# Linear attention on one core: loads cut into 16 pieces on the memory side, 128 on the partition side

## The chip, the core and the metric

The kernel runs on one core of a Trainium2 chip. The engines are TensorE (PE; its weight loads are the row PEld), VectorE (DVE), ScalarE (ACT), GpSimd (POOL) and SyncE (SP); SP computes nothing and issues the transfers, which 16 DMA engines carry out. The metric is the device time of one execution in microseconds (us), the median over several runs; lower is better.

## The reference

For each of 32 heads, q, k and v are 2048 x 128 in bf16:

```python
phi_q = jnp.where(q > 0, q + 1, jnp.exp(q)) + 1e-6
phi_k = jnp.where(k > 0, k + 1, jnp.exp(k)) + 1e-6
kv = jnp.einsum("bhsd,bhse->bhde", phi_k, v)
z = jnp.einsum("bhsd->bhd", phi_k)
num = jnp.einsum("bhqd,bhde->bhqe", phi_q, kv)
den = jnp.einsum("bhqd,bhd->bhq", phi_q, z)[..., None] + 1e-6
return num / den
```

## The kernel before

One head's q, k or v is 512 KB, contiguous in memory. `rows` (L303) lays it over the 128 partitions: partition p holds tokens 16p to 16p+15, which are 2048 elements or 4 KB, contiguous in memory and in the partition. The output goes back the same way. So a head costs three loads and one store of 512 KB each, each made of 128 pieces of 4 KB on both sides.

phi(x) is computed as max(x, 0) + min(exp(x), 1) + 1e-6. For k, ACT makes the exponential `ek_sb` (L368), POOL the positive part `rk_sb` (L372), DVE `emk_sb` = min(ek, 1) + 1e-6 (L382). Five of the 16 tiles of 128 tokens get the two halves added on POOL (L390); for the others PE multiplies both halves. PE sums phi_k by v into `kvz_ps` (L413, L320), with a column of ones beside v that gives z, and ACT copies the result to `kvs_sb` (L430). For q, PE transposes 16 tiles into `xT_ps` (L436), ACT takes the exponential `eq_sb` (L447), DVE and ACT half the positive part each, `rq_sb` (L456, L454), and DVE makes `emq_sb` (L468). PE multiplies both by `kvs_sb` into `o_ps` (L483, L484), and DVE takes the denominators (L506), their reciprocals (L512) and divides (L517, L524) into `o_sb`. The last two heads divide partly on ACT (L536).

The program is written as a list of operations, each with its engine, a key (a number in units of heads), what it reads and what it writes. Every engine runs its own operations in the order of their keys; waits follow from the reads and writes. Nothing decides the order at run time.

All loads (L361) and stores (L571) are issued by SP, in one queue, in the order of these keys:

```python
load("k", k_sb, kf, h - NBI - (1.0 if h < 3 else 1.85 if h == 3 else 1.95))
load("v", v_sb, vf, h - NBI - 0.8)
load("q", q_sb, qf, h - NBI - 0.9)
late = h + 1.0 + 0.18 * h
```

`NBI` is 6: q, k and v have six buffers each, and SP waits until a buffer's readers are done before it issues the load that fills it again. The output has ten buffers (`NBO`), and the stores fall behind their heads by `0.18 * h`, so that the loads go first. The last head but two is stored in three transfers of 51, 13 and 64 partitions (`PARTS`, L252); the last head in two, of tiles 0 to 8 and 9 to 15.

Of the kernel before, what the change touches and what calls it, by code (L numbers as in the profile page):

```python
# [7 lines left out]
P = 128  # L8
# [4 lines left out]
def _ap(base: bass.AP, elem_offset: int, dims):  # L13
    return bass.AP(base.tensor, base.offset + elem_offset, [list(base.ap[0])] + [list(d) for d in dims])
# [217 lines left out]
def bass_standalone__linear_attn_elu__prompt_kernel(  # L232
# [6 lines left out]
    B, H, S, D = q.shape  # L239
    assert D == P and S == 16 * P  # L240
    NT = 16
# [13 lines left out]
    EVEN, ODD = tuple(range(0, NT, 2)), tuple(range(1, NT, 2))  # L255
    MORE = (4, 6, 8, 10, 12, 14)
    GAP = 32
    VW = NT * D + GAP

    qf = q.rearrange("b h s d -> (b h) s d")  # L260
# [4 lines left out]
    with ExitStack() as es:  # L265
        def sb(name, shape, dt):
            return es.enter_context(nc.sbuf_tensor(name, shape, dt))

        k_sb = sb("k_sb", [P, NBI, NT * D], bf16)
        v_sb = sb("v_sb", [P, NBI, VW], bf16)  # L270
        q_sb = sb("q_sb", [P, NBI, NT * D], bf16)
# [29 lines left out]
        pl = Plan()  # L301

        def rows(x, h):  # L303
            return x[h].rearrange("(p j) d -> p (j d)", j=NT)
# [11 lines left out]
               reads=[("id0",)], writes=[("ident",)])  # L316
        pl.add("pool", -7, lambda g: g.memset(_ap(vfull, 0, [[VW, NBI], [1, GAP]]), 1.0), writes=[("vones",)])

# [32 lines left out]
        for h in range(NH):  # L351
# [3 lines left out]
            bi, b2, b3, bo = h % NBI, h % 2, h % 3, h % NBO  # L355

            def load(name, buf, src, key, h=h, bi=bi):
                dst, rws = buf[:, bi], rows(src, h)
                if name == "v":
                    dst = v_sb[:, bi, GAP:]  # L360
                pl.add("sp", key, lambda sp: sp.dma_start(dst, rws), writes=[(name, bi)] + ([("vo", bi)] if name == "v" else []), dma=(name, bi))  # L361

            load("k", k_sb, kf, h - NBI - (1.0 if h < 3 else 1.85 if h == 3 else 1.95))
            load("v", v_sb, vf, h - NBI - 0.8)
            load("q", q_sb, qf, h - NBI - 0.9)

            pl.add("act", at("ek", -2.8),
                   lambda a, bi=bi, b2=b2: a.activation(ek_sb[:, b2, :], k_sb[:, bi, :], ACT.Exp),  # L368
# [36 lines left out]
            def kv(pe, tiles, start=False, stop=False, h=h, bi=bi, b3=b3, both_of=both_of):  # L405
                for j in tiles:
                    both = j in both_of or (j in ODD and j not in ADD and h > 0)
                    for src in (emk_sb, rk_sb) if both else (rk_sb,):
                        first, fin = start and j == tiles[0] and src is (emk_sb if both else rk_sb), stop and j == tiles[-1] and src is rk_sb
                        w = src[:, b3, j * D:(j + 1) * D]  # L410
                        l = j == 0 or (j in ODD and h > 0)
                        c = GAP + j * D
                        last = pe.matmul(kvz_ps[:, 1 - l:NC], lhsT=w, rhs=v_sb[:, bi, c - l:c + D], start=first, stop=fin,  # L413
# [11 lines left out]
            if h:  # L425
                pl.add("pool", h + 0.6, lambda g, bi=bi: g.memset(_ap(vfull, bi * VW + GAP + D - 1, [[2 * D, NT // 2], [1, 1]]), 1.0),
                       reads=[("v", bi)], writes=[("vo", bi)], kind="vo")
# [187 lines left out]
```

## Time and profile before

| | |
|---|---|
| median of 3 runs | 168.16 us (167.96 to 168.21) |
| the profiled execution | 167.82 us |
| its span, first to last instruction | 166.5 us |
| PE / DVE / ACT / POOL busy | 156.0 / 152.3 / 155.0 / 106.3 us |
| granted TensorE clock, mean | 0.997 |
| moved by DMA | 67.25 MB, mean 404 GB/s over the span |
| read from / written to memory | 50.33 / 16.78 MB |

Busy times are of the profiled execution. A share of DMA is the time of its packets as a share of 16 engines; packets of one engine overlap a little, so it can pass 1. "Issue to landing" is the time from SP's instruction to the last of a transfer's 16 semaphore increments.

### The profile page before, as it was taken

How to read it: one execution, taken by the hardware profiler on the slowest of the kernel's cores; microseconds unless marked ns; L12 is line 12 of the kernel's file. 1: busy time of each engine (PE TensorE's matmuls, PEld its weight loads, DVE VectorE, ACT ScalarE, POOL GpSimd, SP SyncE). 2: the span in 40 equal slices, each digit the busy share in tenths (PEclk: the TensorE clock that was granted, in tenths of full speed). 3: DMA queues.
4: the chain of work that ended last, by engine and by line, in shares of the span. 5: the costliest groups of instructions: out<-in, count | busy, mean ns of one | idle time of the engine just before them, and what ended most of it. 6: DMA issues, size and time to landing. Idle time of an engine off the chain costs nothing.

```text
span 166.5 us, 6269 instructions
## 1 busy us (share of the span) xinstructions
PE 156.0 (94%) x2819; PEld 145.3 (87%) x2453; DVE 152.3 (91%) x270; ACT 155.0 (93%) x143; POOL 106.3 (64%) x128
## 2 busy tenths in 40 slices
PE   7789999999999999999999999999999999999960
PEld 0259999999999999899999989999998999999950
DVE  0587999999999999999999999999999999999991
ACT  3979999999999999999999999999999999998790
POOL 2405788676767877676778867676787767677300
PEclk9999999999999999999999999999999999999998
DMA  5999999999999999999999999999999999999986
GB/s 205 345 417 421 413 415 419 412 407 418 417 416 419 422 417 417 422 421 411 424 420 414 423 421 415 419 421 415 422 420 416 422 421 418 418 421 418 415 310 239
DMA packets 18605, 67.25 MB, mean 404 GB/s; under 512 B 2082, under 2 KB 2210, under 8 KB 18594
## 3 DMA queue, kind: packets, MB, share of 16 engines
q1 hardware_dynamic: 18592, 67.12, 99.4%
q8 instruction: 5, 0.08, 0.2%
q14 instruction: 6, 0.05, 0.1%
q10 hardware_dynamic: 2, 0.00, 0.0%
HBM read 50.33 MB, written 16.78 MB: 403 GB/s over the span
## 4 chain that ended last, share of the span: by engine, by line
DVE 58%; PE 17%; POOL 12%; ACT 6%; issue 3%; DMA 2%; DVEq 0%
DVE o_sb L524 20%; POOL rk_sb L390 12%; DVE rq_sb L456 11%; DVE emk_sb L382 10%; DVE emq_sb L468 9%; PE kvz_ps L413 6%; PE o_ps L483 5%; PE o_ps L484 5%; ACT ek_sb L368 3%; DVE rden_sb L512 3%; DVE o_sb L517 3%; ACT eq_sb L447 2%; DMA k_sb<-in_k_dram 2%; DVE den_sb L506 2%; DVE rk_sb L390 1%
## 5 line engine op out<-in xcount | busy, mean ns | idle before, releaser
L413 PE MATMUL kvz_ps<-v_sb,rk_sb 128*128 128x129 bf16 (+1 forms) x512 | 67.0, 220 | 2.8 <-DVE rk_sb L390 1.0
L524 DVE TENSOR_TENSOR o_sb<-o_ps,rden_sb 128x768 bf16<-128x768 f32 (+2 forms) x62 | 67.8, 1135 | 0.0
L390 POOL TENSOR_TENSOR rk_sb<-rk_sb,emk_sb 128x640 bf16<-128x640 bf16 x30 | 41.9, 1395 | 39.5 <-DVE emq_sb L468 38.2
L372 POOL TENSOR_SCALAR rk_sb<-k_sb 128x1024 bf16<-128x1024 bf16 (+1 forms) x60 | 64.1, 1068 | 2.5 <-DMA k_sb<-in_k_dram 2.5
L483 PE MATMUL o_ps<-kvs_sb,emq_sb 128*128 128x129 bf16 (+1 forms) x536 | 65.2, 217 | 0.0
L484 PE MATMUL o_ps<-kvs_sb,rq_sb 128*128 128x129 bf16 (+1 forms) x536 | 64.4, 217 | 0.0
L368 ACT ACTIVATE ek_sb<-k_sb 128x2048 bf16<-128x2048 bf16 x32 | 61.0, 1907 | 2.6 <-DMA k_sb<-in_k_dram 2.6
L447 ACT ACTIVATE eq_sb<-xT_ps 128x2048 bf16<-128x2048 bf16 (+1 forms) x33 | 60.0, 1821 | 2.0 <-PE xT_ps L436 2.0
L413 PE MATMUL kvz_ps<-v_sb,emk_sb 128*128 128x129 bf16 (+1 forms) x338 | 53.3, 221 | 0.6 <-DVE emk_sb L382 0.3
L413 PEld LDWEIGHTS kvz_ps<-v_sb,rk_sb 128*128 128x128 bf16 x512 | 46.1, 98 | 7.6 <-POOL rk_sb L390 2.7
L483 PEld LDWEIGHTS o_ps<-kvs_sb,emq_sb 128*128 128x128 bf16 x536 | 51.2, 98 | 0.8 <-issue 0.3
L484 PEld LDWEIGHTS o_ps<-kvs_sb,rq_sb 128*128 128x128 bf16 x536 | 51.3, 98 | 0.0
L436 PE MATMUL xT_ps<-ident,q_sb 128*128 128x128 bf16 x512 | 33.8, 219 | 0.6 <-DMA q_sb<-in_q_dram 0.4
L436 PEld LDWEIGHTS xT_ps<-ident,q_sb 128*128 128x128 bf16 x512 | 29.9, 98 | 5.1 <-DMA q_sb<-in_q_dram 4.2
L413 PEld LDWEIGHTS kvz_ps<-v_sb,emk_sb 128*128 128x128 bf16 x338 | 32.5, 98 | 0.9 <-DVE emk_sb L382 0.5
L320 PE MATMUL kvz_ps<-ones_sb,rk_sb 128*128 128x1 bf16 x232 | 31.3, 165 | 0.0
L454 ACT ACTIVATE rq_sb<-xT_ps 128x1024 bf16<-128x1024 bf16 x30 | 30.9, 1029 | 0.0
L382 DVE TENSOR_SCALAR emk_sb<-ek_sb 128x2048 bf16<-128x2048 bf16 x32 | 22.0, 688 | 5.6 <-ACT ek_sb L368 5.6
L456 DVE TENSOR_SCALAR rq_sb<-xT_ps 128x1024 bf16<-128x1024 bf16 x34 | 23.3, 690 | 1.1 <-PE o_ps L484 1.0
L468 DVE TENSOR_SCALAR emq_sb<-eq_sb 128x2048 bf16<-128x2048 bf16 x32 | 22.1, 690 | 0.0
L320 PE MATMUL kvz_ps<-ones_sb,emk_sb 128*128 128x1 bf16 x121 | 19.9, 166 | 0.0
L430 ACT ACTIVATE kvs_sb<-kvz_ps 128x129 bf16<-128x129 f32 x32 | 9.0, 281 | 1.6 <-PE kvz_ps L413 0.9
(28 smaller groups left out, 49.2 us busy)
## 6 DMA issues: line engine op xcount, KB each, us to landing
k_sb<-in_k_dram SPq DMA_DIRECT2D x32, 512.0 KB, 15.0
q_sb<-in_q_dram SPq DMA_DIRECT2D x32, 512.0 KB, 15.1
v_sb<-in_v_dram SPq DMA_DIRECT2D x32, 512.0 KB, 15.1
out_dram<-o_sb SPq DMA_DIRECT2D x30, 512.0 KB, 15.3
out_dram<-o_sb SPq DMA_DIRECT2D x1, 288.0 KB, 3.7
out_dram<-o_sb SPq DMA_DIRECT2D x1, 256.0 KB
out_dram<-o_sb SPq DMA_DIRECT2D x1, 224.0 KB, 3.6
out_dram<-o_sb SPq DMA_DIRECT2D x1, 204.0 KB
```

The costliest lines, as they stand in the source:

```text
L320: return pe.add_instruction(mybir.InstMatmult(start_tensor_calc=start, stop_tensor_calc=stop, ldweights=False, bass_skip_group_check=True, ...
L368: lambda a, bi=bi, b2=b2: a.activation(ek_sb[:, b2, :], k_sb[:, bi, :], ACT.Exp),
L372: pl.add(eng, key, lambda e: e.tensor_scalar(rk_sb[:, b3, c], k_sb[:, bi, c], BIG, 0.0, op0=ALU.min, op1=ALU.max), reads=[("k", bi)] + ([( ...
L382: lambda d, b2=b2, b3=b3: d.tensor_scalar(emk_sb[:, b3, :], ek_sb[:, b2, :], 1.0, EPS, op0=ALU.min, op1=ALU.add),
L390: return e.tensor_tensor(out=a, in0=a, in1=b, op=ALU.add)
L413: last = pe.matmul(kvz_ps[:, 1 - l:NC], lhsT=w, rhs=v_sb[:, bi, c - l:c + D], start=first, stop=fin, skip_group_check=True)
L436: last = pe.transpose(xT_ps[:, j * P:(j + 1) * P], q_sb[:, bi, j * P:(j + 1) * P], ident[:])
L447: halves[part] = pl.add("act", key, lambda a: a.activation(eq_sb[:, b2, c], xT_ps[:, c], ACT.Exp), reads=both[part:part + 1] or both, writ ...
L456: f = lambda d: d.tensor_scalar(rq_sb[:, b3, c], xT_ps[:, c], 0.0, None, op0=ALU.max)
L483: pe.matmul(o_ap, lhsT=emq_sb[:, b3, t * P:(t + 1) * P], rhs=kvs_sb[:, b3, c0:c1], start=True, stop=False)
L484: return pe.matmul(o_ap, lhsT=rq_sb[:, b3, t * P:(t + 1) * P], rhs=kvs_sb[:, b3, c0:c1], start=False, stop=True)
L524: pl.add("dve", key, lambda d: d.tensor_tensor(out=o_sb[:, bo, 3 * g0:3 * g1, :].rearrange("p (a b) d -> p a b d", b=3), in0=_ap(full, bas ...
```

## The change

The loads of q, k and v are issued with an access pattern of their own on each side. In memory a head is now 16 pieces of 32 KB (`READS` = 16), each of which is what 8 neighbouring partitions hold; on the partition side there are 128 pieces of 4 KB as before. The same bytes go to the same places. The instruction is made directly (`InstDMACopy`), so that the two patterns stay as written. The stores are unchanged, and on every engine the instructions, their order and their waits are the same; lines below L258 move by 1, those below the load by 8.

```diff
     GAP = 32
+    READS = 16
     VW = NT * D + GAP
...
             def load(name, buf, src, key, h=h, bi=bi):
-                dst, rws = buf[:, bi], rows(src, h)
-                if name == "v":
-                    dst = v_sb[:, bi, GAP:]
-                pl.add("sp", key, lambda sp: sp.dma_start(dst, rws), writes=[(name, bi)] + ([("vo", bi)] if name == "v" else []), dma=(name, bi))
+                row = v_sb[:, bi, GAP:] if name == "v" else buf[:, bi]
+                step, n = row.ap[0][0], P // READS
+                dst = bass.AP(row.tensor, row.offset, [[step, P], [1, NT * D]])
+                whole = src[h]
+                rws = bass.AP(whole.tensor, whole.offset, [[n * NT * D, READS], [1, n * NT * D]])
+
+                def f(sp):
+                    return sp.add_instruction(mybir.InstDMACopy(
+                        mode="Copy", queue="qSPDynamicHW", name=nc.get_next_instruction_name(), engine=mybir.EngineType.SP,
+                        ins=sp.lower_ap_dma(rws), outs=sp.lower_ap_dma(dst)))
+                pl.add("sp", key, f, writes=[(name, bi)] + ([("vo", bi)] if name == "v" else []), dma=(name, bi))
```

## The prediction

> **What bounds the kernel now.** I read the page first, for its queues, its chain and its DMA issues (the last column is us from issue to landing):
>
> ```profile
> q1 hardware_dynamic: 18592, 67.12, 99.4%
> ...
> DVE 58%; PE 17%; POOL 12%; ACT 6%; issue 3%; DMA 2%; DVEq 0%
> ...
> k_sb<-in_k_dram SPq DMA_DIRECT2D x32, 512.0 KB, 15.0
> ```
>
> Two things are full at once. The chain that ended last is compute (DMA has 2% of it), and yet the one queue keeps all 16 engines at work for 99.4% of the span; a load lands 15 us after its issue, having stood behind some twelve others. So I asked the list of waits who ever waits for a load, in the first 17 us and from there to 163 us (first lines of the second answer):
>
> ```profile
> PEld xT_ps L436 <- DMA q_sb<-in_q_dram: 4.2, 1, 4.2
> ACT ek_sb L368 <- DMA k_sb<-in_k_dram: 2.6, 2, 1.5
> POOL rk_sb L372 <- DMA k_sb<-in_k_dram: 2.5, 1, 2.5
> ...
> POOL rk_sb L390 <- DVE emq_sb L468: 38.2, 29, 1.5
> PEld kvz_ps L413 <- POOL rk_sb L390: 2.7, 11, 0.3
> ```
>
> Only the first heads wait for loads. After 17 us nobody does: subtracting landings from first uses in the trace, k lands 3.8 to 5.5 us ahead of its exponential from head 8 on, and q 3.1 to 4.9 us ahead of its transposes. Per-stage rates tell how much room is behind that (columns: stretch, length, busy times, clock, DMA share, GB/s):
>
> ```profile
> 20.00:150.00 130.00, 128.26 (x2402) 124.30 (x2103) 127.46 (x220) 128.56 (x110) 93.49 (x109) 1.00 1.03 418
> 158.00:159.00 1.00, 0.97 (x18) 0.80 (x15) 0.96 (x3) 0.83 (x4) 0.00 (x0) 1.00 1.02 401
> 159.00:159.50 0.50, 0.44 (x9) 0.44 (x10) 0.43 (x4) 0.50 (x4) 0.00 (x0) 1.00 0.97 336
> 159.50:160.50 1.00, 1.00 (x23) 1.00 (x21) 1.00 (x3) 1.00 (x6) 0.00 (x0) 1.00 0.95 295
> 160.50:161.00 0.50, 0.50 (x11) 0.40 (x7) 0.43 (x4) 0.43 (x3) 0.00 (x0) 1.00 0.63 238
> 161.00:162.00 1.00, 0.08 (x2) 0.00 (x0) 0.97 (x4) 0.97 (x4) 0.00 (x0) 1.00 0.58 238
> ```
>
> From 20 to 150 us the engines are at 98% and the queue at 418 GB/s: both limits lie on each other. The queue is idle only near 161, where the shares 0.63 and 0.58 leave 0.5 x 0.37 + 1.0 x 0.42 = 0.6 us. **So a faster load can gain next to nothing, and time added to every load comes out at the end nearly whole, less 0.6 us.** The 3 to 5 us by which loads run ahead are no further cover: the stores queue in the same line, and what makes loads late makes the last stores late too.
>
> The row to keep in mind is 159.50: the share is high, yet 295 GB/s move instead of 418. This is where the store of 64 partitions (the last of the three parts at L252) drains. In the trace's packet records a 4 KB packet takes 159 ns in the median from 20 to 150 us; between 159.1 and 160.5 us, 25 of them take over 250 ns, 341 on average. A transfer's rate hangs on how its partitions are dealt over the engines: 16 engines on half the partitions get in each other's way at 341 / 159 = 2.1 times the packet time.
>
> **The change, part by part.** *Instructions.* Each load remains one instruction at the same place in SP's queue; no wait, order or byte count changes on any engine. The 96 loads are what changes: 96 x 0.524 MB at 418 GB/s, 1.25 us each, 120 us of the queue's time. The stores stay.
>
> *Read side.* 16 read packets per load in place of 128. The trace has 8 KB packets (instruction fetches): 309 ns in the median, against 2 x 159 for two of 4 KB, so a boundary costs 9 ns. Seven fewer on each engine would be worth 63 ns a load, 96 x 0.063 = 6.0 us of queue time. But 128 writes remain, and no row tells which side the 9 ns belongs to: between 0 and -6.0 us. I take 0, because the rows that have 4 KB writes all show 159 ns. Even -6.0 us would hardly show, being hidden by compute (rival 3).
>
> *Issue.* SP takes 0.39 us to issue the first load and 0.42 to 0.47 for the next ones while nothing blocks it. Fewer pieces may bring this down by up to 0.2 us, more decoding could add as much; only the first one stands on the path, before 3.34 us of load. I take 0.
>
> *Write side.* This decides. A 32 KB piece is what 8 neighbouring partitions hold, so an engine that reads a piece must write partitions 8e to 8e+7, one after the other. Before, with 128 pieces on both sides, the dealing was free, and the steady 159 ns show that the one in use is without collisions. The trace of before has no load dealt in eights; its bounds are the full-width transfers (factor 1.0) and the half-width store (factor 2.1). I lean to the upper one because all 16 engines step through their eight partitions together, so what they touch at one moment is partitions 0, 8, 16, ... and not an even cover. How much in step? The first 16 packets of the kernel begin between 1.86 and 2.08 us; 0.22 us out of a load's 8 x 159 ns = 1.27 us is 0.17 of it, so 0.83 of the time collides, which at twice the time gives 1.83. Random spacing would leave a half: 1.5. Single engines are knocked out of step now and then (five instruction packets of 16 KB took 0.93 to 0.98 us, 8 KB ones 0.31), but a load has landed only when its last engine has. I take 1.75.
>
> [...]
>
> **The sum.** 1.25 us x 0.75 = 0.94 us more per load, x 96 = 90.0 us, less 0.6 us of idle queue = +89.4 us. 167.82 us (profiled) + 89.4 = 257.2; the median of the runs lies 0.34 us higher than the profiled execution: 257.6 us, told as 258. What is late next: the exponential and the transposes of each head wait for k and q, every compute engine idles over a third of the time, and the buffers no longer gate SP.
>
> **The rivals.** About 0.2% (0.34 us) is what a measurement of this kernel can tell from no change.
>
> 1. *Nothing happens*, 168.2 us (167.8 to 168.5): all 128 partitions are still reached, so the cover is full on average and small buffers even out the rest; or the pieces are cut back to 4 KB and dealt as before, the change not doing what it says. For it: the full-width transfers all run at 159 ns. Against it: the half-width store shows that averages do not help when engines meet. Chance 0.08. [...]
>
> 2. *The engines fall out of step and stay so.* Whoever is served first runs ahead until its neighbour writes elsewhere; then collisions are short. Factor 1.05 to 1.3: 120 x 0.05 = 6 to 120 x 0.3 = 36 us, less 0.6: 173 to 204 us. For it: once apart, nothing in the queue brings engines together, and there are always some twelve transfers lined up. Against: the 25 slow packets all sit near twice the time, as if shared evenly, not served by turns of whole packets. Chance 0.12.
>
> 3. *Faster.* No collisions, and the 9 ns come off. The place is the start: in the chain up to 21 us only the first k load (0.73 to 4.07 us) is DMA, and it would land 0.06 us earlier; the second q lands at 10.22 us, 0.31 us earlier as the fifth load, but PE is busy until 10.14 and starts at 10.31, so 0.06 + 0.17 = 0.23 us is all: 167.9 us. It passes 0.34 us only if the first load's latency also shrinks by over 0.1 us (its first packets took 205 to 444 ns); then 167.6. The end gives nothing: the last divide ends at 162.84 us and its store is unchanged. Chance 0.04.
>
> 4. *Slightly slower*: only the start pays, 169 to 172 us, if 32 KB reads begin to write later or instruction fetches wait longer for their turn; 0.02.
>
> **How the numbers follow.** Collisions at 1.3 to 2.1 (204 to 300 us) have 0.74; the likeliest value is 258. The range 180 to 296 us takes in nearly all of that and most of rival 2, leaving out the unchanged cases, which are 0.12, and some 0.08 at its ends. Faster 0.04; same 0.08, rival 1; slower 0.88: the forecast 0.74, rival 2 0.12, rival 4 0.02.
>
> **What would show it.** Right: 4 KB packets near 280 ns in loads, the stretch 20 to 150 us at a DMA share of 1 or more but near 268 GB/s (2.1 MB, a head's four transfers, in 3 x 2.19 + 1.25 = 7.8 us), the chain mostly DMA from k and q, and PE and ACT busy for about the same 156 us in a span of 257. Wrong: 418 GB/s or more in that stretch, and no wait for loads after 17 us. A rate of 340 to 400 GB/s would be rival 2.

## The result, and the profile after

The changed kernel takes 215.83 us (median of 4 runs, 213.37 to 217.06) against 168.08 us before (167.96 to 168.21). It is slower by 47.8 us. The two slower of its four runs count as slow and are left out of the ratio, which is 1.274 with a 95% interval of 1.270 to 1.279 (213.37 and 214.94 us against 168.08). Its profiled execution took 216.72 us, with a span of 215.3. Lines of the load and below have moved by 8: `xT_ps` is L444, `kvz_ps` L421.

The page after: busy times, queue and chain.

```profile
PE 165.0 (77%) x2819; PEld 150.9 (70%) x2453; DVE 162.4 (75%) x270; ACT 159.1 (74%) x143; POOL 108.7 (50%) x128
...
q1 hardware_dynamic: 7840, 67.12, 98.4%
...
DMA 65%; PE 12%; SPq 9%; DVE 8%; issue 2%; POOL 1%
DMA q_sb<-in_q_dram 53%; DMA v_sb<-in_v_dram 12%; SPq L366 5%; SPq L579 4%; PE kvz_ps L421 4%; PE xT_ps L444 4%; DVE o_sb L532 3%; PE o_ps L491 2%; PE o_ps L492 2%; DVE emq_sb L476 2%; DVE rq_sb L464 1%; PE o_ps L321 1%; DVE rden_sb L520 1%; POOL rk_sb L398 1%; DVE emk_sb L390 1%
```

The chain has turned over: DMA from 2% to 65%, nearly all of it loads of q and v, and DVE from 58% to 8%. The queue moves the same 67.12 MB in 7840 packets instead of 18592 (the records count reads: 96 x 16 now, 96 x 128 before) and still fills the span. The engines do the same work; PE's busy time is longer, which goes with a granted clock of 0.953 on average, not 0.997. DVE's is longer too, 162.4 us in place of 152.3; no run says why.

The list of waits from 17 to 200 us, where before none was for a load:

```profile
PE xT_ps L444 <- DMA q_sb<-in_q_dram: 16.7, 18, 2.0
...
PE kvz_ps L421 <- DMA v_sb<-in_v_dram: 7.7, 12, 1.9
```

And the stages (stretch, length, busy times, clock, DMA share, GB/s):

```profile
20.00:50.00 30.00, 21.83 (x358) 20.77 (x315) 22.08 (x38) 20.95 (x19) 15.25 (x18) 0.89 0.99 243
50.00:150.00 100.00, 80.87 (x1422) 76.06 (x1243) 79.93 (x129) 78.45 (x66) 57.12 (x66) 0.97 1.01 324
```

The same stretches before the change:

```profile
20.00:50.00 30.00, 29.64 (x557) 28.76 (x489) 29.35 (x53) 29.65 (x26) 21.04 (x25) 1.00 1.03 416
50.00:150.00 100.00, 98.62 (x1849) 95.54 (x1616) 98.11 (x168) 98.90 (x85) 72.45 (x85) 1.00 1.03 419
```

There are two stages, which the prediction did not have. From 20 to 50 us the share is 1 at 243 GB/s; from 50 to 150 us it is 324 GB/s, and rising (304 up to 100 us, 344 up to 150, 356 up to 200). In the trace's packet records the 32 KB reads take 2.12 us on average up to 50 us, 1.22 us at the fastest later on, and 1.752 us over the run. The border is where the first stores get their turn: the first one is issued at 24.13 us, and no 4 KB packet moves before 54.9.

### The profile page after: what moved, and what is told of

The parts are those of the page before. It is cut to its first block, busy times and chain, and to the rows that moved or that the text cites. A ratio compares the mean times of both kernels' runs of the same rounds, so it can differ in the third digit from the quotient of the medians.

```text
span 215.3 us, 6269 instructions
## 1 busy us (share of the span) xinstructions
PE 165.0 (77%) x2819; PEld 150.9 (70%) x2453; DVE 162.4 (75%) x270; ACT 159.1 (74%) x143; POOL 108.7 (50%) x128
## 3 DMA queue, kind: packets, MB, share of 16 engines
q1 hardware_dynamic: 7840, 67.12, 98.4%
## 4 chain that ended last, share of the span: by engine, by line
DMA 65%; PE 12%; SPq 9%; DVE 8%; issue 2%; POOL 1%
DMA q_sb<-in_q_dram 53%; DMA v_sb<-in_v_dram 12%; SPq L366 5%; SPq L579 4%; PE kvz_ps L421 4%; PE xT_ps L444 4%; DVE o_sb L532 3%; PE o_ps L491 2%; PE o_ps L492 2%; DVE emq_sb L476 2%; DVE rq_sb L464 1%; PE o_ps L321 1%; DVE rden_sb L520 1%; POOL rk_sb L398 1%; DVE emk_sb L390 1%
## 5 line engine op out<-in xcount | busy, mean ns | idle before, releaser
L455 ACT ACTIVATE eq_sb<-xT_ps 128x2048 bf16<-128x2048 bf16 (+1 forms) x33 | 60.1, 1824 | 18.8 <-PE xT_ps L444 18.6
L421 PE MATMUL kvz_ps<-v_sb,emk_sb 128*128 128x129 bf16 (+1 forms) x338 | 55.2, 225 | 20.1 <-issue 11.5
L491 PE MATMUL o_ps<-kvs_sb,emq_sb 128*128 128x129 bf16 (+1 forms) x536 | 67.4, 221 | 0.0
L492 PE MATMUL o_ps<-kvs_sb,rq_sb 128*128 128x129 bf16 (+1 forms) x536 | 66.6, 221 | 0.4 <-issue 0.4
L421 PE MATMUL kvz_ps<-v_sb,rk_sb 128*128 128x129 bf16 (+1 forms) x512 | 66.4, 224 | 0.2 <-POOL rk_sb L398 0.2
L492 PEld LDWEIGHTS o_ps<-kvs_sb,rq_sb 128*128 128x128 bf16 x536 | 52.4, 100 | 0.6 <-issue 0.6
L491 PEld LDWEIGHTS o_ps<-kvs_sb,emq_sb 128*128 128x128 bf16 x536 | 52.6, 100 | 0.1
L444 PE MATMUL xT_ps<-ident,q_sb 128*128 128x128 bf16 x512 | 34.7, 222 | 21.0 <-DMA q_sb<-in_q_dram 19.8
L421 PEld LDWEIGHTS kvz_ps<-v_sb,emk_sb 128*128 128x128 bf16 x338 | 33.5, 101 | 24.1 <-issue 24.1
L444 PEld LDWEIGHTS xT_ps<-ident,q_sb 128*128 128x128 bf16 x512 | 30.1, 99 | 28.3 <-issue 21.7
L421 PEld LDWEIGHTS kvz_ps<-v_sb,rk_sb 128*128 128x128 bf16 x512 | 47.5, 101 | 2.4 <-issue 1.4
L434 POOL MEMSET v_sb<- 128x8 bf16 x31 | 5.3, 171 | 50.9 <-PE kvz_ps L321 50.9
L390 DVE TENSOR_SCALAR emk_sb<-ek_sb 128x2048 bf16<-128x2048 bf16 x32 | 25.4, 792 | 7.1 <-ACT ek_sb L376 7.1
L321 PE MATMUL kvz_ps<-ones_sb,rk_sb 128*128 128x1 bf16 x232 | 30.1, 169 | 0.0
L476 DVE TENSOR_SCALAR emq_sb<-eq_sb 128x2048 bf16<-128x2048 bf16 x32 | 26.1, 817 | 0.0
```

Source lines behind the costliest of these rows:

```text
L321: return pe.add_instruction(mybir.InstMatmult(start_tensor_calc=start, stop_tensor_calc=stop, ldweights=False, bass_skip_group_check=True, ...
L444: last = pe.transpose(xT_ps[:, j * P:(j + 1) * P], q_sb[:, bi, j * P:(j + 1) * P], ident[:])
L455: halves[part] = pl.add("act", key, lambda a: a.activation(eq_sb[:, b2, c], xT_ps[:, c], ACT.Exp), reads=both[part:part + 1] or both, writ ...
L476: lambda d, b2=b2, b3=b3: d.tensor_scalar(emq_sb[:, b3, :], eq_sb[:, b2, :], 1.0, EPS, op0=ALU.min, op1=ALU.add),
L491: pe.matmul(o_ap, lhsT=emq_sb[:, b3, t * P:(t + 1) * P], rhs=kvs_sb[:, b3, c0:c1], start=True, stop=False)
L492: return pe.matmul(o_ap, lhsT=rq_sb[:, b3, t * P:(t + 1) * P], rhs=kvs_sb[:, b3, c0:c1], start=False, stop=True)
```

## The experiments

Theory A is that of the prediction: how a load's partitions are dealt over the engines decides, and with 16 pieces engines meet while writing. Theory B: long reads are slow in themselves. "Dealt in eights" is the name here for 16 pieces, each of which holds eight neighbouring partitions; "in fours" is that for 32 pieces, of four partitions each, and in theory A for 128 as well. The trace's records name neither engine nor partition of a packet: which partitions an engine gets, and that engines meet there, is my assumption, and the runs show the times alone. The kernels dealt in eights scatter: most differ by 4 to 20 us from run to run, so that small differences between them say nothing.

**32 pieces of 16 KB.**

```diff
-    READS = 16
+    READS = 32
```

> The changed kernel with 32 pieces of 16 KB on the memory side in place of 16 of 32 KB; all else as changed. Theory A (dealing: with 16 pieces an engine must write 8 neighbouring partitions, and engines then meet; with 32 pieces an engine can again take two groups of four partitions, as with 128 pieces): no collisions, 16 KB reads at some 610 ns (2 x 309 of the 8 KB packets, less a boundary of 9), 20 to 150 us at 420 to 435 GB/s, time 167.6 to 168.4 us, as before the change. Theory B (size: long reads are slow in themselves, whoever writes what): a part of the 48 us remains with reads half as long, 180 to 210 us.

Measured: 168.32 us (12 runs), before 167.98 (17 runs), ratio 1.003 (1.000 to 1.006). The stages:

```profile
20.00:50.00 30.00, 29.76 (x558) 28.81 (x490) 29.41 (x52) 29.75 (x27) 20.81 (x25) 1.00 1.01 418
50.00:150.00 100.00, 98.63 (x1849) 95.54 (x1616) 98.08 (x169) 98.90 (x85) 72.45 (x85) 1.00 1.01 423
```

The 48 us are gone, and 423 GB/s is a little above the 419 of the same stretch before. The median 16 KB read took 615 ns. Reads of 16 KB did no harm.

**4 KB reads with an outer count of 16.**

```diff
-                dst = bass.AP(row.tensor, row.offset, [[step, P], [1, NT * D]])
+                dst = bass.AP(row.tensor, row.offset, [[step, P], [NT * D, 1], [1, NT * D]])
...
-                rws = bass.AP(whole.tensor, whole.offset, [[n * NT * D, READS], [1, n * NT * D]])
+                rws = bass.AP(whole.tensor, whole.offset, [[n * NT * D, READS], [NT * D, n], [1, NT * D]])
```

> The memory side has 16 x 8 pieces of 4 KB (outer count 16, as in the changed kernel; reads of 4 KB, as before the change). Theory A: the dealing goes by the outer count of 16, so engines meet as in the changed kernel; 4 KB packets of loads at 160 to 310 ns, mean near 220; time 210 to 225 us. Theory B: reads are short again, so 168 us.

Measured: 211.97 us (206.56 to 214.33, 4 runs).

```profile
20.00:50.00 30.00, 21.15 (x350) 20.16 (x304) 21.33 (x33) 20.37 (x19) 15.61 (x17) 0.89 1.03 240
50.00:150.00 100.00, 78.61 (x1384) 73.80 (x1206) 79.30 (x127) 76.51 (x63) 55.81 (x64) 0.97 1.03 317
```

Reads are as short as before the change, and the loss is there, in both stages. Their 4 KB packets take 278 to 288 ns on average in each 5 us between 5 and 40 us, and 206 over the run (stores included). B falls: the outer count of 16 costs the time, and the size of the reads at most a few us of it. The two runs together are the cleanest pair of the study. What they do not part is the two sides of a load. If an engine takes one of the 16 parts, it also reads 32 KB of neighbouring memory, here as in the changed kernel; that engines meet at the partitions and not in memory is argued, and no run changes one side alone.

**Half the partitions at a time.**

```diff
+                n, H2 = P // 2 // READS, P // 2
...
                 def f(sp):
...
+                    for i in range(2):
+                        to = bass.AP(row.tensor, row.offset + i * H2 * step, [[step, H2], [1, NT * D]])
+                        fr = bass.AP(whole.tensor, whole.offset + i * H2 * NT * D, [[n * NT * D, READS], [1, n * NT * D]])
...
```

> Every load is issued as two transfers, of partitions 0 to 63 and 64 to 127, each of 16 pieces of 16 KB: an engine writes four neighbouring partitions, and 16 engines write into half the partitions at any time. Theory A (upper bound of the prediction, 2.0 to 2.1 times): 16 KB reads near 1210 to 1250 ns, a load 2.45 to 2.6 us, time 168 + 96 x (1.2 to 1.35) - 0.6 = 283 to 297 us. Theory B: reads of 16 KB, so no slower than the changed kernel, at most 216 us.

Measured: 211.22 us (two runs, 206.55 and 215.9), far from 283.

```profile
20.00:50.00 30.00, 20.85 (x350) 19.94 (x307) 21.58 (x33) 20.08 (x19) 14.81 (x17) 0.89 1.01 238
50.00:150.00 100.00, 81.04 (x1479) 76.12 (x1290) 83.46 (x135) 81.72 (x67) 59.99 (x68) 1.00 1.01 339
```

The upper bound of the prediction was wrong. The time fits theory B's bound too, but B has fallen by the two runs above. A 16 KB read takes 1.09 us up to 50 us (1.77 times the 615 ns), and 863 ns over the run (1.40 times, as in the changed kernel). With 32 pieces over all partitions, reads of the same size took 615 ns: the loss came back when each transfer reached half the partitions, which speaks for the partition side. Why the second stage, stores included, moves 339 GB/s and the first 238, no run shows.

**Putting engines apart by hand.** My assumption here, which no record shows, was that engines meet in pairs while in step, so that four of them held back by half a load would be free of their partners. First, two small transfers ahead of all loads, of 12 and of 4 partitions, into a scratch tile:

```diff
+        for i, n in enumerate((12, 4)):
+            def lag(sp, i=i, n=n):
+                to, fr = x_sb[0:n, i], vf[0, 0:n * NT].rearrange("(p j) d -> p (j d)", j=NT)
...
+            pl.add("sp", -20 + i, lag, writes=[("x", i)], dma=("x", i))
```

> [...] Theory B: 217 to 219 us.

Measured: 207.64 us (205.83 to 215.08). The lag did not come about as meant: the small packets took 160 to 336 ns and were done before the first load's packets began at 3.75 us. Neither range of time, 172 to 200 us if spacing helps and 217 to 219 if it does not, holds the 207.6 us. That load's reads differed (1.40 to 2.14 us), and the second load's were all alike again, 2.05 to 2.09. So I put the lag into a full queue, behind the first v load, with four pieces of 16 KB and then of 8 KB, meant to hold back four engines:

```diff
+        def lag(sp):
+            to = bass.AP(x_sb[:, :].tensor, x_sb[:, :].offset, [[4 * x_sb[:, :].ap[0][0], 4], [1, 4 * NT * D]])
+            fr = vf[0, 0:4 * 4 * NT].rearrange("(p j) d -> p (j d)", p=4)
...
+        pl.add("sp", -6.5, lag, writes=[("x", 0)], dma=("x", 0))
```

> [...]

> [...]

Measured: 198.26 us and 209.09 us, one run each. The lag came about and lasted. In the seven loads behind the 16 KB, five of a load's 16 reads begin 1.1 to 1.5 us after the first, about half a load late; behind the 8 KB the 16 begin within 0.94 us, and in the changed kernel within 0.56. Yet all 16 reads of these loads take nearly the same time, 2.0 to 2.2 us; eight at 1.2 to 1.4 (to 1.8 behind the 8 KB) and eight at 2.1, which I expected of pairs, were never seen. That two engines meet as a pair, and are free when spaced, is not borne out, and neither is the rival, that step is restored: the reads took its 2.0 to 2.2 us, but their starts stayed apart. The 16 KB took 1.06 us, which is seven packets at 159 ns but half a load at the 2.1 us that loads took there; the 8 KB took 0.54 us. The 198 us stand alone, and no cause was found for them.

**Do the stores help?** Stores cut to one tile of 16, so that loads have the queue to themselves:

```diff
-                pl.add("sp", key, lambda sp: sp.dma_start(rows(of, h)[p0:p1, t0 * D:t1 * D],
-                                                          o_sb[p0:p1, bo, t0:t1].rearrange("p j d -> p (j d)")),
+                pl.add("sp", key, lambda sp: sp.dma_start(rows(of, h)[p0:p1, t0 * D:(t0 + 1) * D],
+                                                          o_sb[p0:p1, bo, t0:t0 + 1].rearrange("p j d -> p (j d)")),
```

> The changed kernel, each store cut to its first tile of 16 (the rest of the output is not written), so that the queue holds loads dealt in eights and next to nothing else. Theory C (stores, dealt in fours, shake the engines out of step, which is why reads quicken after the first stores): 32 KB reads stay near 2100 ns to the last load, time 96 x 2.1 + 14 = 210 to 220 us, although 15 MB less are moved. Theory D (the engines drift apart with time, stores or not): reads fall to 1300 to 1600 ns after 50 us, time 170 to 185 us.

Measured: 200.6 us, two runs far apart (191.1 and 210.1), with a quarter less to move. The profile is of the longer one:

```profile
20.00:50.00 30.00, 21.68 (x345) 20.85 (x302) 20.32 (x33) 20.01 (x19) 15.30 (x17) 0.83 0.97 229
50.00:150.00 100.00, 80.44 (x1466) 75.53 (x1277) 89.23 (x135) 81.53 (x67) 58.73 (x68) 1.00 1.02 270
```

There, reads go from 2.2 us to 1.85 to 2.07 after 50 us and stay there (mean of the run 1.98), where the changed kernel's fall to 1.23 at times. So some quickening comes without stores, and in this run less than with them. The other run was 19 us shorter; spread over 96 loads that makes, as an estimate, reads near 1.78 us, hardly above the changed kernel's 1.752. How much the stores do is therefore not shown. Stores dealt in eights as well (16 x 8 pieces of 4 KB in memory):

```diff
...
+                    to = bass.AP(whole.tensor, whole.offset, [[n * NT * D, READS], [NT * D, n], [1, NT * D]])
...
```

> The changed kernel, with the 512 KB stores dealt in eights as well (16 x 8 pieces of 4 KB in memory, 128 on the partition side). Theory C1 (it is the other dealing of the stores that brings the loads out of step): 32 KB reads stay at 1900 to 2100 ns after 50 us, time 235 to 280 us. Theory C2 (any store does it, because an engine on a store writes nothing into the partitions and leaves the others room): reads fall to a mean below 1800 ns as in the changed kernel, time 205 to 225 us.

Measured: 208.95 us (two runs), 345 GB/s from 50 to 150 us, reads 1.40 to 1.77 us on average in each 25 us from 50 us on. C1 falls: the quickening does not hang on stores being dealt otherwise than loads. C2's ranges hold, but that any store brings the quickening is not shown: by the run before, time alone may do it.

**Stores alone dealt in eights**, by the same edit to the kernel before:

> The kernel before, with only the 512 KB stores dealt in eights (16 x 8 pieces of 4 KB in memory, 128 on the partition side); loads as before. If reading partitions for a store and writing them for a load do not meet, only stores meet stores, and a store mostly has loads around it: a store's packets at 160 to 300 ns, 0 to 30 us of queue time, 168 to 195 us, and load packets at 159 ns. If they do meet: load packets slow down too, as in the kernel that changes k alone, 200 us or more.

Measured: 168.58 us (8 runs) against 167.94 (9), ratio 1.003 (1.000 to 1.006), and in the stages:

```profile
50.00:150.00 100.00, 98.68 (x1850) 95.56 (x1616) 98.10 (x169) 98.95 (x85) 72.46 (x85) 1.00 1.03 419
```

At most 0.6% for the 15.7 MB of these stores. But in this trace one of them does pay. The last load lands at 150.7 us, and the stores that follow each other in the full queue run at the old rate. The last 512 KB store is issued at 160.79 us into a queue that has nearly run empty (a share of 0.30 from 161.5 to 162 us); where it drains, 51 of the 4 KB packets take over 250 ns, against 1 to 7 in the kernel before and in the two with 32 pieces. First the kernel before, then this one (stretch, length, clock, DMA share, GB/s):

```profile
151.00:158.00 7.00, 1.00 1.03 418
162.00:164.50 2.50, 1.00 0.99 384
...
151.00:158.00 7.00, 1.00 1.03 418
162.00:164.50 2.50, 1.00 0.98 292
```

This is a sign that the edit did change the dealing, and that such a store is not free as such. In the full queue it cost nothing, where loads dealt in eights run at 243 GB/s at first; what saves the stores there, no run shows.

**k alone.**

```diff
-                step, n = row.ap[0][0], P // READS
+                step, reads = row.ap[0][0], READS if name == "k" else P
+                n = P // reads
...
```

> Only the loads of k have 16 pieces of 32 KB; q and v have 128 pieces on both sides, as before the change. Proportion: a third of the 48 us, 184 us. Theory C (transfers dealt in fours between them shake the engines out of step): k reads at 1220 to 1600 ns, mean below 1500, so at most 32 x 0.25 = 8 us more: 168 to 176 us.

Measured: 217.83 us (215.76 to 225.0, 4 runs): with a third of the loads changed, all of the loss. Both expectations fail.

```profile
20.00:50.00 30.00, 23.73 (x413) 22.75 (x359) 22.99 (x36) 22.37 (x20) 15.70 (x19) 0.94 1.00 278
50.00:150.00 100.00, 77.37 (x1368) 72.45 (x1193) 77.42 (x128) 78.22 (x64) 54.98 (x62) 0.98 1.03 322
```

The packet records say how. The k reads take 1.83 us on average, 32 x (1.83 - 1.25) = 18.6 us. But the 4 KB packets, q, v and stores, now take 199 ns where they took 160: 12160 of them over 16 engines, 760 x 39 ns = 29.6 us. Together 48.2 of the 49.7 us. Why the q, v and store packets slow down beside k loads, no record shows.

**What queue time costs.** Six loads more in the kernel before, into scratch:

```diff
+            if h in EXTRA:
+                i = EXTRA.index(h)
+                pl.add("sp", h - NBI - 0.85, lambda sp, i=i, h=h: sp.dma_start(x_sb[:, i], rows(qf, h)), writes=[("x", i)], dma=("x", i))
```

> The kernel before, with six loads more (of q, 512 KB each, into scratch tiles nobody reads), one beside the loads of heads 8, 12, 16, 20, 24 and 28. Theory (the prediction's cover): queue time comes out at the end but for 0.6 us of idle queue, 6 x 1.25 - 0.6 = 6.9 us more: 174 to 176 us. Rival: the 3 to 5 us by which loads run ahead of their use hide it: 168 to 172 us.

Measured: 175.62 us against 168.16, ratio 1.045 (1.038 to 1.053): 7.5 us for 6 x 1.25 = 7.5 us of queue. The lead of the loads is no cover; the interval, 6.4 to 8.8 us, holds the 6.9 of the theory and not the rival's 4. Its list of waits has the sign of it, from 17 to 200 us:

```profile
PE kvz_ps L418 <- DMA v_sb<-in_v_dram: 3.3, 4, 1.7
```

**16 KB reads after the start.** With 32 pieces throughout, SP took 0.57 us to issue the first load, not 0.39, and it landed 0.31 us later. So the first three heads keep their 128 pieces:

```diff
-    READS = 16
+    READS = 32
...
+                if h < 3:
+                    dst, rws = v_sb[:, bi, GAP:] if name == "v" else buf[:, bi], rows(src, h)
...
+                    return
```

> 16 KB reads (32 pieces) from head 3 on, the first three heads loaded as before the change. With 32 pieces throughout, the first k load landed at 4.38 us in place of 4.07 (SP took 0.57 us to issue it in place of 0.39) and the time was 0.3 us above the kernel before. If that start is all of it: the first k lands at 4.1 us, 20 to 150 us at 423 GB/s, time 167.7 to 168.1 us, not to be told from the kernel before. If long reads cost something later: 168.3 us again.

Measured: 167.61 us (12 runs) against 168.17 (17), ratio 0.9964 (0.9939 to 0.9989): the only version that beats the kernel before, by 0.4%, and just below the expected 167.7 to 168.1. The first k lands at 4.05 us as expected, and the stretch from 50 to 150 us runs at 423 GB/s, that from 20 to 50 at 419. Its profiled execution took 168.58 us, above that median, so the profile does not show where the 0.6 us come from.

## Why the prediction was right, and where its size was off

*The bound.* Right. Loads made longer came out at the end whole, in the changed kernel and with the six extra loads. Three details of what is late next were wrong: the chain waits for q and v, not k and q; PE, DVE and ACT idle for 23 to 26% of the span, not over a third; and SP still waits for readers of buffers before it issues loads, some 33 us in all by its list of waits, against 29 before.

*Dealing, not size.* Right: the two runs that part the outer count from the length of the reads (168.32 and 211.97 us) settle it. The forecast case, a factor of 1.3 to 2.1, is the one that came, at 1.40 near its lower edge; the measured 215.8 us lie 42 us under the likeliest 258, in a range 116 us wide. That the engines meet at the partitions stays argued.

*The factor* is the term that was mis-sized: "I take 1.75". Measured over the run it is 1.752 us / 1.25 us = 1.40. With that the sum closes: 96 x (1.752 - 1.25) = 48.2 us, less 0.6, is 47.6; measured were 47.8 between the medians and 48.9 between the profiled executions. The 1.75 is near what loads alone show (2.12 / 1.25 = 1.69 up to 50 us; there the stage ran at 243 GB/s, and I had foreseen 268 for loads and stores together). What I left out is that the factor falls in the course of the run: after 50 us it is 1.64 / 1.25 = 1.31. Stores between the loads may be a part of this (1.98 us per read without them in the profiled run, 1.75 with them), but the two runs without stores lie too far apart to say. Rival 2, engines falling out of step, has a factor of up to 1.3 and describes the second stage better than the forecast does, but the rate there, 324 GB/s, is below the 340 to 400 I gave it.

*Rival 1.* Its reading, that it is enough if a load reaches all partitions, falls: all 128 are written by every load, at 243 GB/s from 20 to 50 us.

*The upper bound* of 2.1, from the half-width store at the end of the kernel before, did not carry over to loads in a full queue, and neither did the doubled time of a collision that the 1.83 is made from: 1.77 at worst, 1.40 on average. And my argument for the lean, 16 engines in step by 0.83, is not borne out: with the starts of a load's reads spread over up to 1.5 us, behind the lag, all 16 were as slow. That the 1.75 came near the 1.69 of the first stage is luck.

*Read side.* I took 0 of 0 to -63 ns per load. The fastest 32 KB reads took 1.216 us against 8 x 159 ns = 1.272 us, and 16 KB reads 615 against 636 ns. So a boundary that goes on the read side saves 7 to 8 ns of the 9, 56 ns a load. As forecast it hardly shows in the time. *Issue.* I took 0 of ±0.2 us, a bound that no row gave; it was +0.24 us (0.63 us for the first load).

What stays open: why in the first stage all 16 reads of a load take the same 2.0 to 2.2 us, spaced or not; whether they meet at the partitions or in memory; what loosens that later, stores or time; and what makes the runs of most kernels dealt in eights differ by 4 to 20 us where the kernel before keeps within 3.

## What to carry to other kernels

Before widening a DMA's pieces on one side, ask which share each engine then gets: with an outer count of 16 each load of a saturated queue took 40% longer (1.752 us for 1.25), and the 4 KB packets of the other transfers slowed as well (199 ns for 160 with k alone changed). Half the widening (16 KB, 32 pieces) kept the queue's full rate, 423 GB/s. Where a queue and the engines are full at the same time, queue time counts although nobody waits for it: six loads of 1.25 us cost 7.5 us.

## What the runs showed of the hardware that I had not expected

- Stores dealt in eights cost nothing while the queue was full (418 GB/s, 4 KB packets at 159 ns in the median), loads did. The one such store that began on a nearly empty queue was slow as well (292 GB/s where 384 ran before).
- Dealing a third of the loads badly cost as much as dealing all of them so (217.8 and 215.8 us).
- SP took 0.56 to 0.63 us to issue a load made directly as `InstDMACopy`, against 0.39 to 0.47 for `dma_start`. The number of pieces is not the reason: with k alone changed, the loads of q have 128 pieces on both sides, and the first ones took 0.57 to 0.59 us.
- Of the 9 ns of a packet boundary, 7 to 8 ns are saved for each one that goes on the read side alone (615 ns for 16 KB, 1216 for 32 KB, with the writes still in pieces of 4 KB).
